# A tuned attention and feed-forward kernel: phi summed on VectorE straight from PSUM, its eps folded into a sums column, and x loaded ahead of the weights

## Chip, cores, metric

The kernel runs on one core of a Trainium2 chip. The metric is the device time of one execution in microseconds (us); lower is better. All runs quoted are fast, with a mean granted TensorE clock between 0.995 and 1.0 in every timed run. Within that band the clock and the time still go together a little: of the 31 runs of the kernel before that were timed beside the experiments, the nine at 0.997 or less have a median of 532.22 us and the 21 at 0.999 or more one of 531.42. A difference of under 1 us between two kernels is therefore not read as one here. In what follows PE is TensorE, DVE VectorE, ACT ScalarE, POOL GpSimd and SP the engine that issues the DMAs (SPq in the page's list of them).

## The reference, cut to what matters

Linear attention and a gated feed-forward layer work side by side on one layer-normalised input: 2048 tokens, D = 576, 32 heads of 18, F = 4608.

```python
xn  = layernorm(x)
q, k, v = split(xn @ wqkv)                                # 32 heads of 18
phi = lambda t: where(t > 0, t + 1, exp(t)) + 1e-6
kv  = einsum("bhsd,bhse->bhde", phi(k), v);  z = phi(k).sum(tokens)
o   = (phi(q) @ kv) / (phi(q) @ z + 1e-6)
out = x + o @ wo + (gelu(xn @ w_gate) * (xn @ w_up)) @ w_down
```

Two identities carry the kernel. First, phi(t) without its eps is max(t, 0) + exp(min(t, 0)), and min(t, 0) is -relu(-t). Second, V is never built: kv = (xn' phi(k))' Wv, so the kernel accumulates the Gram matrix G = xn' phi(k) over all tokens in PSUM.

## The kernel before

The work falls into a prologue of some 78 us (layer norm, K, Gram, Q, then kv) and a feed-forward stretch of some 450 us. The prologue is one tile loop over 16 tiles of 128 tokens, whose instructions are issued in the order of a hand-made plan of times. The kernel lays PSUM out as 8 banks (`ps_all` of 128 x 8 x 512). In the tile loop before, Gram takes banks 0 to 4, K banks 5 and 6, Q bank 7.

```python
def k_relu(n, hf=None):                       # ACT: e = relu(-k), both K banks in one (576 columns)
    ps, e, _ = k_part(n, hf)
    nc.scalar.activation(out=e, in_=ps, func=ACT.Relu, scale=-1.0)
def k_max(n, hf=None):                        # DVE: a = max(k, 0) + eps; the K banks are free after this
    ps, _, a = k_part(n, hf)
    nc.vector.tensor_scalar(out=a, in0=ps, scalar1=0.0, scalar2=EPS_ATT, op0=ALU.max, op1=ALU.add)
def k_exp(n):                                 # ACT: e = exp(-e)
    e = k_ea[n][0]
    nc.scalar.activation(out=e[:], in_=e[:], func=ACT.Exp, scale=-1.0)
def k_add(n):                                 # POOL: phi(k) = e + a, for the Gram step
    e, a = k_ea.pop(n)
    (nc.gpsimd if n < NS - 1 else nc.vector).tensor_tensor(out=pk[:, n, :], in0=e[:], in1=a[:], op=ALU.add)

G_A = {0: [...], 1: [...], 2: [...], 4: [...]}    # four of five row blocks of G in the loop, banks 0 to 4
G_B = {3: [(5, 0, 0, 288), (6, 0, 288, 288)]}     # the fifth in a pass of its own, at the end
q_banks = _Ring([7])                              # one bank for the q units of the loop
TILE = 3.34                                       # us per tile in the plan
# ...
# after the loop: q pairs (12,13) (15,16) (17,18) (14,19), then the G_B pass, its copies, z and kv
```

The step of phi(q) was like that of k, with a POOL add; some units had another form on DVE. [...] marks cuts.

## Time and profile before

| | before |
|---|---|
| time, median of 3 (range) | 532.21 us (531.52 to 532.48) |
| span of the profiled run | 529.3 us |
| first gate/up matmul, the end of the prologue | 78.43 us |
| PE / DVE / ACT / POOL busy, whole span | 98 / 49 / 27 / 13% |

The prediction below shows the page and the timeline. Two views more say where PE is held up. The first is the page's chain of work that ended last, by engine, and the second the busy time by stages: each row has the stretch in us, its length, then the busy time of an engine with its number of instructions.

```profile
PE 88%; DVE 5%; ACT 3%; POOL 1%; DMA 1%; issue 0%; SPq 0%; ACTq 0%; POOLq 0%; DVEq 0%
```

```profile
core 0: us, PE busy (x) PEld busy (x) DVE busy (x) ACT busy (x) POOL busy (x), PEclk, DMA share, GB/s
14.36:62.94 48.58, 45.60 (x340) 33.82 (x340) 39.02 (x75) 34.95 (x72) 32.24 (x33) 1.00 0.52 119
78.43:529.30 450.87, 447.18 (x3942) 261.82 (x3940) 194.59 (x280) 89.50 (x154) 24.62 (x26) 1.00 0.37 107
```

The chain leaves PE for 12% of the span, mostly through DVE, ACT and POOL, and nearly all of that lies in the prologue (from 80 us on, DVE's part of the chain is 0.1%). The first stage is the tile loop from the first Gram step to the last: DVE is busy for 39 of 48.6 us, POOL for 32. A PE figure near 94% says little here, since matmul records overlap: the Gram step at 15.96 in the prediction's first timeline ends by its record at 17.11 (15.96 + 1.15), while the next group of matmuls starts at 16.94.

### The profile page before, as it was taken

What the parts mean: (1) busy time and instruction counts of PE and PEld (TensorE: products, weight loads), DVE (VectorE), ACT (ScalarE), POOL (GpSimd) and SP (SyncE); (2) the same over time, 40 slices, a digit from 0 to 9 for tenths busy, and PEclk for the clock granted to TensorE, in tenths of its full rate; (3) what the DMA queues carried; (4) which work ended last, traced back from release to release, by engine and by line L of the source; (5) the groups of instructions that cost most, each with busy time, mean ns of one, the idle gap of its engine ahead of it and who ended that gap; (6) DMA issues with size and microseconds to landing.
All of it is one profiled execution on the core that took longest, in us unless ns stands there. A gap on an engine that the chain in (4) does not pass through costs nothing.

```text
span 529.3 us, 10714 instructions
## 1 busy us (share of the span) xinstructions
PE 518.7 (98%) x4530; PEld 315.1 (60%) x4530; DVE 257.5 (49%) x407; ACT 142.9 (27%) x266; POOL 66.7 (13%) x80
## 2 busy tenths in 40 slices
PE   7999999999999999999999999999999999999997
PEld 6766664555577764444577744444677544445775
DVE  7888683877338613433368233433485233433110
ACT  5777662232340003323200023323000123322000
POOL 3667440121002200000012000000021000000000
PEclk9999999999999999999999999999999999999999
DMA  8474205899610025555400055555100355540000
GB/s 256 118 153 122 71 1 163 246 265 267 174 53 12 24 74 146 156 154 156 135 11 13 12 163 158 143 161 150 49 22 12 101 146 161 144 134 1 12 12 24
DMA packets 106954, 57.89 MB, mean 109 GB/s; under 512 B 13402, under 2 KB 106522, under 8 KB 106906
## 3 DMA queue, kind: packets, MB, share of 16 engines
q1 hardware_dynamic: 106906, 57.21, 38.3%
q8 instruction: 35, 0.57, 0.5%
q14 instruction: 13, 0.11, 0.1%
HBM read 52.86 MB, written 2.36 MB: 104 GB/s over the span
## 4 chain that ended last, share of the span: by engine, by line
PE 88%; DVE 5%; ACT 3%; POOL 1%; DMA 1%; issue 0%; SPq 0%; ACTq 0%; POOLq 0%; DVEq 0%
PE ps_all L336 54%; PE ps_all L675 27%; PE ps_all L680 4%; DVE phi_a L409 1%; PE ps_all L306 1%; DVE xn L225 1%; DVE pqT L421 1%; PE ps_all L254 1%; POOL hT L291 1%; DMA x_sb<-in_A_x_dram 1%; ACT phi_e L279 1%; PE ps_all L366 1%; ACT phi_e L287 1%; DVE stats L215 1%; PE ps_all L472 1%; DVE phi_a L283 1%
## 5 line engine op out<-in xcount | busy, mean ns | idle before, releaser
L336 PE MATMUL ps_all<-xnT,wg 64*128 64x512 bf16 x1152 | 272.6, 376 | 0.0
L336 PE MATMUL ps_all<-xnT,wu 64*128 64x512 bf16 x1152 | 271.7, 376 | 0.0
L646 DVE TENSOR_TENSOR hT<-ps_all,gl 128x512 bf16<-128x512 f32 x144 | 99.6, 691 | 164.6 <-ACT gl L645 164.1
L645 ACT ACTIVATE gl<-ps_all 128x512 f32<-128x512 f32 x144 | 86.1, 598 | 317.2 <-PE ps_all L336 297.8
L336 PEld LDWEIGHTS <-wu 64*128 64x128 bf16 x1152 | 108.3, 94 | 66.2
L336 PEld LDWEIGHTS <-wg 64*128 64x128 bf16 x1152 | 108.3, 94 | 65.8
L675 PE MATMUL ps_all<-wd_sb,hT 128*128 128x288 bf16 x1152 | 147.0, 286 | 0.0
L675 PEld LDWEIGHTS <-hT 128*128 128x128 bf16 x1152 | 112.3, 98 | 30.6 <-issue 1.3
L496 DVE RECIPROCAL den_sb<-den_sb 126x128 f32<-126x128 f32 (+1 forms) x80 | 68.3, 911 | 0.5
L499 POOL TENSOR_TENSOR pqT<-pqT,den_sb 126x512 bf16<-126x512 bf16 (+3 forms) x25 | 24.2, 966 | 302.7 <-DVE den_sb L496 282.4
L683 DVE TENSOR_TENSOR res<-ps_all,x_sb 128x288 bf16<-128x288 f32 x32 | 14.7, 458 | 88.0 <-PE ps_all L680 88.0
L336 PE MATMUL ps_all<-xnT,wr 64*128 64x512 bf16 x288 | 55.1, 376 | 0.0
L680 PE MATMUL ps_all<-m_sb,pqT 126*128 126x288 bf16 (+1 forms) x160 | 24.9, 286 | 0.0
L336 PEld LDWEIGHTS <-wr 64*128 64x128 bf16 x288 | 14.5, 94 | 16.8 <-issue 0.7
L254 PE MATMUL ps_all<-wqkv_sb,xnT 128*128 128x288 bf16 x160 | 22.9, 286 | 1.4 <-DVE phi_a L283 1.2
L306 PE MATMUL ps_all<-hT,xn 128*128 128x288 bf16 (+3 forms) x192 | 22.4, 266 | 1.6 <-POOL hT L291 0.8
L291 POOL TENSOR_TENSOR hT<-phi_e,phi_a 128x576 bf16<-128x576 f32 x15 | 21.5, 1434 | 13.5 <-DVE phi_a L283 7.3
L306 PEld LDWEIGHTS <-xn 128*128 128x128 bf16 (+1 forms) x192 | 18.1, 101 | 6.5 <-issue 3.1
L254 PEld LDWEIGHTS <-xnT 128*128 128x128 bf16 x160 | 15.0, 98 | 7.5 <-issue 1.1
L680 PEld LDWEIGHTS <-pqT 126*128 126x128 bf16 (+1 forms) x160 | 15.5, 97 | 4.1
L419 POOL TENSOR_TENSOR pqT<-phi_e,phi_a 126x512 bf16<-126x512 f32 (+1 forms) x12 | 15.6, 1298 | 15.1 <-DVE phi_a L409 8.1
L409 DVE TENSOR_SCALAR phi_a<-ps_all 126x512 f32<-126x512 f32 (+1 forms) x20 | 13.3, 678 | 5.2 <-ACT phi_e L402 4.8
(65 smaller groups left out, 205.7 us busy)
## 6 DMA issues: line engine op xcount, KB each, us to landing
wg<-in_B_w_gate_dram SPq DMA_DIRECT2D x72, 256.0 KB, 2.9
wu<-in_B_w_up_dram SPq DMA_DIRECT2D x72, 256.0 KB, 3.5
wd_sb<-in_B_w_down_dram SPq DMA_DIRECT2D x12, 432.0 KB, 4.4
wr<-in_B_w_gate_dram SPq DMA_DIRECT2D x72, 32.0 KB, 2.7
wr<-in_B_w_up_dram SPq DMA_DIRECT2D x72, 32.0 KB, 3.0
out_dram<-res SPq DMA_DIRECT2D x15, 144.0 KB, 1.8
x_sb<-in_A_x_dram SPq DMA_DIRECT2D x3, 576.0 KB, 6.0
wqkv_sb<-in_A_wqkv_dram SPq DMA_DIRECT2D x2, 576.0 KB, 5.9
```

The costliest lines, as they stand in the source:

```text
L254: nc.tensor.matmul(ps_all[:, k_bank(n, hf), :HALF], lhsT=xnT[:, kt, n * P:(n + 1) * P], rhs=wqkv_sb[:, kt, D + hf * HALF:D + (hf + 1) * HALF],
L291: (nc.gpsimd if n < NS - 1 else nc.vector).tensor_tensor(out=pk[:, n, :], in0=e[:], in1=a[:], op=ALU.add)
L306: nc.tensor.matmul(ps_all[:m, b, col:col + w], lhsT=xn[:, n, j0:j0 + m], rhs=pk[:, n, d0:d0 + w], start=(n == 0 and col == 0), stop=(n == ...
L336: return nc.tensor.matmul(self.outs[i], lhsT=self.lhs(i, rows, kt), rhs=self.rhs(i, rows, kt), start=start, stop=stop, skip_group_check=True,)
L409: nc.vector.tensor_scalar(out=a, in0=ps, scalar1=0.0, scalar2=one + EPS_ATT, op0=ALU.max, op1=ALU.add)
L419: nc.gpsimd.tensor_tensor(out=out_, in0=e, in1=a, op=ALU.add)
L496: nc.vector.reciprocal(out=d[:, h:h + P], in_=d[:, h:h + P])
L499: nc.gpsimd.tensor_tensor(out=pqT[:rows, c, cols], in0=pqT[:rows, c, cols], in1=d, op=ALU.mult)
L645: nc.scalar.activation(out=gl[:], in_=ps_all[:, b[0], :], func=ACT.Gelu_apprx_tanh)
L646: nc.vector.tensor_tensor(out=hT[:, GUB * k + i, :], in0=ps_all[:, b[1], :], in1=gl[:], op=ALU.mult)
L675: nc.tensor.matmul(acc, lhsT=hT[:, f, j * P:(j + 1) * P], rhs=wd_sb[:, f, hs], start=(f == 0), stop=False,)
L680: nc.tensor.matmul(acc, lhsT=pqT[:rows, c, ts_], rhs=m_sb[:rows, c, hs], start=False, stop=(c == NCH - 1),)
```

## The change

The intent is to take POOL out of phi(k), to make PE the only bound of the tile loop, and to start the loop earlier. The diff, cut to its core:

```diff
-    load_x(0, 1); load_x(1, 1); load_wk(0); (last rows of wk); load_x(2, 1); load_wk(1); load_x(3, 1); load_x(4, 4)
+    load_x(0, 1); load_x(1, 1); load_x(2, 2); load_w(1); load_x(4, 2); load_x(6, 2)

-    def k_max(n, hf=None): ...  vector.tensor_scalar(max 0, + eps)
-    def k_exp(n): ...           scalar.activation on 576 columns
-    def k_add(n): ...           gpsimd.tensor_tensor(e + a)
+    def k_exp(n, hf): ...       scalar.activation on 288 columns
+    def k_sum(n, hf):
+        ps, e, out_ = k_part(n, hf)
+        nc.vector.scalar_tensor_tensor(out=out_, in0=ps, scalar=0.0, in1=e, op0=ALU.max, op1=ALU.add)

-    G_A = {0: [...], 1: [...], 2: [...], 4: [...]}           # 576 columns a row block
-    G_B = {3: [...]}
+    G_A = {0: [...], 1: [...], 4: [...]}                     # 577: pk has a column of ones
+    G_B = {2: [(5, 0, 0, 288), (6, 0, 288, 289)], 3: [(0, 0, 0, 288), (1, 0, 288, 289)]}

-    q_banks = _Ring([7])
+    q_banks = _Ring([4, 7])
+    def q_eps(i): ...           gpsimd.tensor_scalar(e * 1 + eps)
+    def q_sum(i): ...           as k_sum, from the q bank

     def g_copy(kt, pieces, on):
+        nc.vector.tensor_scalar_mul(out=eps, in0=ps_all[:m, b, col + w - 1:col + w], scalar1=EPS_ATT)
-        copy(out=g_sb[...], in_=ps_all[...])
+        (ACT Identity with bias eps, or DVE tensor_scalar_add of eps)

-    TILE = 3.34
+    TILE = 2.94                  # and all times of the plan
-    # after the loop: four q pairs, G_B pass, copies, z, kv
+    # after the loop: G_B pass 2, copies, q 12, G_B pass 3, copies, q 13, z, kv, three q pairs
```

The eps of phi(k) reaches G exactly as eps times the row sums of xn. The ones column makes these sums, and the copies out of PSUM add them. The normalised tail columns that are duplicated for the transposes are also copied on DVE instead of POOL from tile 4 on.

## The prediction

Cut is what it said of the hardware that no trace or run shows: one paragraph, with the conclusion that POOL would not hold up the new sums, and some terms that rested on it. The times that the trace before does show are these. A normalisation of 128x576 takes 0.42 to 0.43 us in nine tiles, but 0.96 to 1.71 in six, in each of which it ends 0.16 to 0.18 us after a POOL add of phi(k) does. The gate product over 128x512 from PSUM takes DVE 0.69. Over 126x512, ACT takes 0.59 from PSUM and 0.63 for an exp in SBUF, and POOL 1.27 for its two-input add; it has no one-input operation of that size.

DVE per tile after came to 3.3 us (2.8 with overlaps); the term of the two sums of k is cut from it, and the terms left make 2.4. ACT's 3.4 and 2.7 keep all their terms, but where the 0.44 of an exp came from is cut; the trace before gives 0.44 as an estimate too, since relu takes 0.651 us for 576 columns and 0.405 for 288, and exp 0.683 for 576: 0.683 - (0.651 - 0.405) = 0.437. The overlap of 0.09 shows there as well (an exp from 28.23 to 28.91, the next instruction from 28.82). The forecast itself, 7.8 + 62.5 + 3.2 = 73.5, counts PE's work and stalls and loses no term; that DVE stays under PE's 3.06 per tile rests in part on the term that is cut.

> **What bounds the kernel now.** I read the page first (busy shares, slices), then the busy time by windows, then the chain of waits and the timeline of the first 95 us.
>
> ```profile
> span 529.3 us, 10714 instructions
> PE 518.7 (98%) x4530; PEld 315.1 (60%) x4530; DVE 257.5 (49%) x407; ACT 142.9 (27%) x266; POOL 66.7 (13%) x80
> ...
> PE   7999999999999999999999999999999999999997
> ...
> DVE  7888683877338613433368233433485233433110
> ```
>
> TensorE is busy throughout; VectorE is dense only in the first six slices (some 79 us), which are the attention prologue. The timeline puts the first gate/up matmul at 78.43 us. From there to the last matmul at 525.6 us I compared start times of consecutive matmuls: only 0.1 us is without issue. The change touches nothing of that stretch's PE work, so about 451 us (529.3 - 78.4) are **fixed**. All gain must come from the first 78.4 us. Matmul busy time flatters PE there[...]; start-to-start times tell the true cost:
>
> ```profile
> 15.96 1.15 PE L306 MATMUL ps_all<-hT,xn 128*128 128x288 bf16 x10
> ...
> 16.94 0.78 PE L254 MATMUL ps_all<-wqkv_sb,xnT 128*128 128x288 bf16 x5
> ...
> 17.56 1.15 PE L306 MATMUL ps_all<-hT,xn 128*128 128x288 bf16 x10
> ...
> 58.02 1.26 PE L366 MATMUL ps_all<-xnT,wqkv_sb 128*126 128x512 bf16 x5
> ...
> 59.11 1.39 PE L254 MATMUL ps_all<-wqkv_sb,xnT 128*128 128x288 bf16 x10
> ...
> 71.94 4.09 PE L306 MATMUL ps_all<-hT,xn 128*128 128x288 bf16 x32
> ...
> 75.87 0.42 PE L442 MATMUL ps_all<-zsel,g_sb 128*126 128x126 bf16 x5
> ```
>
> Columns are start, duration, engine and line. A Gram step of 10 matmuls (2304 columns) takes 16.94 - 15.96 = 0.98 us, so 0.425 ns per column; half a K tile 0.62; a Q unit 59.11 - 58.02 = 1.09; the second Gram pass 75.87 - 71.94 = 3.93. **PE work before**, from 7.3 us on: K 16 x 1.23 = 19.6, Gram 16 x 0.98 + 3.9 = 19.6, 12 Q units 13.1, four Q pairs 7.9 (64.07 to 71.94), z and kv some 1.5, transposes 1.0: 62.7. The stretch 7.3 to 78.4 is 71.1 long, so 8.4 us are stalls and spin matmuls, of which I count some 1.5 of stall before the first Gram step, 0.8 of spin and 5.8 of stall after it. What makes the stalls is visible around 33 us:
>
> ```profile
> 29.13 1.40 POOL L291 TENSOR_TENSOR hT<-phi_e,phi_a 128x576 bf16<-128x576 f32 x1 [0.51 <-ACT rstd L221]
> ...
> 29.37 1.34 DVE L225 TENSOR_SCALAR xn<-x_sb,mv,rstd 128x576 bf16<-128x576 bf16 x1 [0.38 <-ACT rstd L222]
> ...
> 32.75 0.75 DVE L283 TENSOR_SCALAR phi_a<-ps_all 128x576 f32<-128x576 f32 x1
> ...
> 33.55 1.39 PE L254 MATMUL ps_all<-wqkv_sb,xnT 128*128 128x288 bf16 x10 [0.60 <-DVE phi_a L283]
> 33.64 1.46 POOL L291 TENSOR_TENSOR hT<-phi_e,phi_a 128x576 bf16<-128x576 f32 x1 [2.63 <-DVE phi_a L283]
> ...
> 35.15 1.15 PE L306 MATMUL ps_all<-hT,xn 128*128 128x288 bf16 x10 [0.22 <-POOL hT L291]
> ```
>
> The normalisation starts under a GpSimd add, ends when that add ends (29.37 + 1.34 = 30.71, against 0.43 when undisturbed) and delays the whole DVE queue; k_max is then late, so the K bank comes free late and PE waits, and PE waits again for the 1.4 us GpSimd add of phi(k). The same pair recurs at 42 to 47 us.
>
> [...]
>
> **The change, part by part.**
> DVE, per steady tile. Before: normalisation 0.79 (mean of 15), statistics 2 x 0.45 + 0.21, k_max 0.75, q_max 0.68, the DVE form of q's last step 0.65 on every third unit, so 0.2: 3.5. After: normalisation 0.43, statistics 1.11, [...]one q sum 0.69, the 64-column copy moved from GpSimd 0.18: 3.3. Successive DVE instructions start some 0.08 before the one ahead ends (0.59 from q_max to the next start, with duration 0.67), so I take 2.8 effective.
> ACT, per tile after: rstd 0.29 + 0.20, two relus of 0.41, two exps of 0.44[...], q 0.59 + 0.63: 3.4, less 8 overlaps of 0.09: 2.7. Before it was some 0.4 less.
> POOL: its adds of 1.43 per K tile and 1.27 per Q unit go; a one-input eps operation per Q unit comes[...]. It never feeds a Gram step again.
> PE, per tile after: K 1.23, Gram 1731 columns x 0.425 = 0.74, Q unit 1.09: 3.06. **PE becomes the bound** at 3.06, with DVE and ACT at 2.7 to 2.8, where before the disturbed chain made a pitch of some 3.67 ((60.34 - 27.30)/9 between Gram starts) against PE's 3.30.
> PE total after: K 19.6, Gram 16 x 0.74 + 2 x 3.93 = 19.7, 14 Q units 15.3, three pairs 5.9, z/kv 1.5, transposes about 1.0: 63.0, 0.3 **more** than before. The eps column adds only 1 column in 577; its eps sums and copies stand beside other PE work. Gram columns move from the tile loop to two full passes later, which removes no work but gives a filler without waits, and the q pairs now come after kv, so the copies of G hide (the 0.8 us kv wait goes).
> Prologue: the normalisation no longer stands behind statistics of x tile 2, which waited for its load and cost 1.4 us of PE time before 7.3. But the K weights now come behind four x tiles.
>
> ```profile
> GB/s 0 17 244 222 252 236 298 325 301 333 371 318 378 346 136 134 30 0 0 163 1 0 164 46 267 349 45 128 71 319 318 96 153 265 149 232 3 49 115 188
> ```
>
> This is the transfer rate per microsecond over the first 40 us. Its sum to 7 us is 1.27 MB. Four x tiles and the K weights are 4 x 0.147 + 0.664 = 1.25 MB, so K can begin at about 7.5 to 8 us, not earlier than now (7.86): the early gain is swallowed by the load, but one Q unit then fits ahead of the first Gram step.
>
> **The sum.** K starts at 7.8. PE work still to do then 62.5 (transposes of the first tile are done). Stalls and spin I expect: 1.0 before the first Gram step, 1.5 in the tile loop, 0.7 in the tail where phi of the last pairs shares ACT with the gelu table load. 7.8 + 62.5 + 3.2 = 73.5 as first gate/up matmul, against 78.4: 4.9 us less, 532.2 - 4.9 = 527.3; I say 527.4.
>
> **Rivals.** (a) The plan works perfectly and PE has nearly no stall: 71 us, total 525. For it: the plan issues at 2.94 per tile, so the other engines run ahead of PE. Against: in the kernel before a plan of 3.34 came out at 3.67. (b) The waits move: ACT takes 0.4 more per tile and more instructions[...]; DVE waits for both exps before the sum frees the K bank. The relu, exp, sum chain now holds the bank where before relu and max did, some 0.5 us longer. If PE keeps 0.25 us of stall per tile, and the tail 1.5, the total is 530 to 531. (c) K weights land late, at 9 to 9.5 us: everything shifts by 1.5, total 529. (d) The last pairs' phi holds banks that gate/up wants: three pairs need 2.2 us of ACT each against 2 us of PE, then 1.28 of table load and GpSimd's eps; a stall of 0.5 to 1.5, total 528 to 529.
>
> **Range and chances.** (a) and the more likely halves of (b) to (d) span 525.2 to 530.4, with run noise of half a microsecond. 2% is 10.6 us; all the non-work of PE in the prologue is 8.4, plus 1.4 before 7.3 that the weights' load keeps: so faster by 2% needs more than there is. Slower by 2% needs twice today's stalls. Chances: faster 0.01, within 0.98, slower 0.01.
>
> **What would show it.** Right if: the first gate/up matmul starts at 72 to 75 us; the last Gram step of the tile loop begins near 55, before it was 62.94; normalisation is about 0.43 in most tiles; [...]the Gram steps have no wait on POOL; first K matmul at 7.5 to 8.2; the stretch after it as long as before. Wrong if: gate/up starts before 71.5 or after 76.5; PE waits in most tiles for ACT's exp or DVE's sum; the normalisation is still blocked in half the tiles, by the eps operation; K starts after 9; a second ACT table load appears for the copies with a bias; or the gate/up stretch itself gains stalls.

## The result

| | before | after |
|---|---|---|
| time, median (range), 4 runs each | 531.87 (530.70 to 532.48) | 525.17 (524.61 to 526.45) |
| profiled run, its span | 531.11, 529.3 | 526.45, 524.7 |
| first gate/up matmul in the profile | 78.43 | 73.41 |
| pitch of the tile loop (mean time from one tile to the next) | 3.67 | 3.05 |

The ratio is 0.988 (95% interval 0.9854 to 0.9906). Ratios are the mean time of one kernel's fast runs over that of the other's of the same rounds, so they differ a little from the ratio of the medians. The change is 6.7 us by the medians. The result is within 2%, as predicted; it is 2.2 us under the 527.4 predicted and 0.03 us under the lower end of the range as it was written. The profiled run of the changed kernel is the slowest of its four.

The page after: span and busy time, the slices of DVE, and the chain by engine.

```profile
span 524.7 us, 10664 instructions
PE 517.2 (99%) x4502; PEld 315.8 (60%) x4502; DVE 248.4 (47%) x426; ACT 147.9 (28%) x301; POOL 40.1 (8%) x63
...
DVE  7887545977348423333388134333584233333110
...
PE 96%; DMA 2%; ACT 1%; DVE 0%; SPq 0%; issue 0%; DVEq 0%
```

PE now carries 96% of the chain, and DVE's part has gone from 5% to nothing. POOL's busy time fell from 66.7 to 40.1 us. DVE's dense part ends earlier. The stages after, in the same columns:

```profile
14.47:54.85 40.38, 39.47 (x291) 29.35 (x290) 32.77 (x91) 36.03 (x99) 6.18 (x10) 1.00 0.54 125
54.85:73.41 18.56, 18.56 (x167) 13.49 (x166) 7.71 (x20) 8.57 (x17) 3.26 (x6) 1.00 0.00 1
73.41:524.70 451.29, 447.59 (x3942) 262.79 (x3938) 197.21 (x282) 94.24 (x163) 27.05 (x30) 1.00 0.38 109
```

The loop took 8.2 us less (48.58 to 40.38). The tail took 3.1 more (78.43 - 62.94 = 15.49 before, 18.56 after), mainly because Gram columns moved into it. The feed-forward stretch is the same within 0.4 us. The sum is -5.0 us at the first gate/up matmul (the start of the first Gram step hardly moved: 14.36 to 14.47). One tile of the loop after, from its timeline (start, duration, engine, line):

```profile
40.80 0.91 PE L294 MATMUL ps_all<-hT,xn 128*128 128x288 bf16 x7
...
41.30 0.77 ACT L274 ACTIVATE phi_e<-phi_e 128x288 f32<-128x288 f32 x2
...
41.55 1.24 PE L347 MATMUL ps_all<-xnT,wqkv_sb 128*126 128x512 bf16 x5
...
41.77 0.82 DVE L278 SCALAR_TENSOR_TENSOR hT<-ps_all,phi_e 128x288 bf16<-128x288 f32 x2
...
42.67 0.62 POOL L389 TENSOR_SCALAR phi_e<-phi_e 126x512 f32<-126x512 f32 x1 [2.38 <-DVE hT L278]
...
43.85 0.91 PE L294 MATMUL ps_all<-hT,xn 128*128 128x288 bf16 x7
...
44.03 0.42 DVE L221 TENSOR_SCALAR xn<-x_sb,mv,rstd 128x576 bf16<-128x576 bf16 x1
...
46.44 0.69 DVE L393 SCALAR_TENSOR_TENSOR pqT<-ps_all,phi_e 126x512 bf16<-126x512 f32 x1 [0.79 <-POOL phi_e L389]
```

From one Gram step to the next it is 43.85 - 40.80 = 3.05 us, what PE alone needs. None of PE's lines here has a wait behind it. The two exps (41.30 to 42.07) are still at work when the first of the two sums starts at 41.77: each half waits for its own exp alone. The normalisation takes 0.42 us, and POOL does one operation of 0.62. Who PE waited for, the three largest before (first fence, from 7 us to 79) and after (second, 7 to 74): total us, times, longest.

```profile
PE ps_all L240 <- DVE xn L225: 1.3, 1, 1.3
PE ps_all L254 <- DVE phi_a L283: 1.2, 2, 0.6
PE ps_all L306 <- POOL hT L291: 0.8, 4, 0.2
```

```profile
PE ps_all L250 <- DMA wqkv_sb<-in_A_wqkv_dram: 0.8, 1, 0.8
PE ps_all L250 <- DMA xnT<-xn: 0.7, 1, 0.7
PE ps_all L236 <- ACT xnT L239: 0.6, 1, 0.6
```

The waits for DVE and POOL are gone, but for one of 0.2 us for a sum at the start of the loop. What is left are two DMA landings, which differ from run to run (the wait for the weights is 0.4 us in a_noeps and a_nocol, that for a transpose 0.3 in a_loads and none in a_nocol), and one copy before the loop. Measured by start times of consecutive matmuls, PE stood still 7.3 us before (from 7.3 to 78.4 us) and 3.2 after (from 7.3 to 73.4), of which 1.8 are the two landings (by the same measure).

### The profile page after: what moved, and what is told of

Same layout as the page of the kernel before. It is cut to its first block, busy times and chain, and to the rows that moved or that the text cites. A ratio compares the mean times of both kernels' runs of the same rounds, so it can differ in the third digit from the quotient of the medians.

```text
span 524.7 us, 10664 instructions
## 1 busy us (share of the span) xinstructions
PE 517.2 (99%) x4502; PEld 315.8 (60%) x4502; DVE 248.4 (47%) x426; ACT 147.9 (28%) x301; POOL 40.1 (8%) x63
## 4 chain that ended last, share of the span: by engine, by line
PE 96%; DMA 2%; ACT 1%; DVE 0%; SPq 0%; issue 0%; DVEq 0%
PE ps_all L318 55%; PE ps_all L664 27%; PE ps_all L669 4%; PE ps_all L294 3%; PE ps_all L250 3%; PE ps_all L347 3%; DMA wqkv_sb<-in_A_wqkv_dram 1%; DMA xnT<-xn 1%; PE ps_all L442 1%; PE ps_all L424 0%; PE ps_all L646 0%; SPq L93 0%; ACT phi_e L270 0%; DVE hT L278 0%; ACT xnT L239 0%; ACT phi_e L274 0%
## 5 line engine op out<-in xcount | busy, mean ns | idle before, releaser
L294 PE MATMUL ps_all<-hT,xn 128*128 128x288 bf16 (+4 forms) x176 | 22.4, 276 | 0.0
L393 DVE SCALAR_TENSOR_TENSOR pqT<-ps_all,phi_e 126x512 bf16<-126x512 f32 (+1 forms) x20 | 13.4, 672 | 12.4 <-POOL phi_e L389 12.4
L347 PE MATMUL ps_all<-xnT,wqkv_sb 128*126 128x512 bf16 (+1 forms) x70 | 17.4, 378 | 0.0
L389 POOL TENSOR_SCALAR phi_e<-phi_e 126x512 f32<-126x512 f32 (+1 forms) x20 | 12.4, 618 | 54.2 <-DVE hT L278 29.8
```

The source lines that it names most:

```text
L294: nc.tensor.matmul(ps_all[:m, b, col:col + w], lhsT=xn[:, n, j0:j0 + m], rhs=pk[:, n, d0:d0 + w], start=(n == 0 and col == 0), stop=(n == ...
L347: nc.tensor.matmul(ps, lhsT=wqkv_sb[:, kt, q0:q0 + rows], rhs=xnT[:, kt, sc * SC:(sc + 1) * SC], start=(kt == 0), stop=(kt == KT - 1),)
L393: nc.vector.scalar_tensor_tensor(out=out_, in0=ps, scalar=0.0, in1=e, op0=ALU.max, op1=ALU.add)
```

## The experiments

Twelve kernels, each timed in 5 rounds beside the kernel before on the same chip; all twelve passed the comparison with the reference. "Before" in the table is the median of the kernel before in the same rounds. The twelve ran in three groups on three chips. The changed kernel was not timed again beside them, so its 525.17 comes from another session; the medians of the kernel before in all sessions lie between 531.41 and 531.87.

| run | based on | time, median (range) | before | ratio (95%) |
|---|---|---|---|---|
| b_sum | before | 533.45 (532.27 to 534.06) | 531.55 | 1.0036 (1.0021 to 1.0052) |
| b_dummy | before | 534.19 (533.33 to 534.38) | 531.55 | 1.0050 (1.0035 to 1.0065) |
| b_half | before | 528.87 (528.36 to 531.30) | 531.57 | 0.9955 (0.9938 to 0.9972) |
| a_pooladd | after | 535.97 (535.52 to 538.13) | 531.55 | 1.0095 (1.0077 to 1.0114) |
| a_whole | after | 533.22 (532.80 to 533.69) | 531.57 | 1.0030 (1.0017 to 1.0043) |
| a_q1 | after | 536.12 (535.72 to 536.69) | 531.57 | 1.0085 (1.0072 to 1.0098) |
| a_wkfirst | after | 526.27 (525.09 to 526.83) | 531.55 | 0.9895 (0.9879 to 0.9912) |
| a_tail | after | 525.75 (525.50 to 526.22) | 531.41 | 0.9894 (0.9872 to 0.9916) |
| a_noeps | after | 525.24 (524.92 to 525.80) | 531.41 | 0.9882 (0.9860 to 0.9904) |
| a_nocol | after | 525.15 (524.40 to 525.47) | 531.41 | 0.9877 (0.9855 to 0.9900) |
| a_loads | after | 524.83 (524.44 to 525.74) | 531.41 | 0.9875 (0.9849 to 0.9901) |
| a_best | after | 525.45 (525.23 to 525.69) | 531.57 | 0.9884 (0.9871 to 0.9897) |

The prediction's theory was that the POOL add (through the normalisations that it holds up, 1.34 us against 0.43, and its place ahead of each Gram step) caused the loop's stalls. The first rival was the new plan.

### b_sum: the sum alone, in the kernel before

```diff
-    def k_max(...): nc.vector.tensor_scalar(out=a, in0=ps, ...)
+    def k_max(...): pass
     def k_add(n):
-        (nc.gpsimd if n < NS - 1 else nc.vector).tensor_tensor(out=pk[:, n, :], in0=e[:], in1=a[:], op=ALU.add)
+        nc.vector.scalar_tensor_tensor(out=pk[:, n, :] (viewed as two halves), in0=ps, scalar=0.0, in1=e, op0=ALU.max, op1=ALU.add)
-   k_add times [10.08, 12.33, 14.18, 16.88, ..   k_half 1: 13.33   k_relu 1: 14.06
+   k_add times [10.08, 12.13, 14.18, 16.60, ..   k_half 1: 14.20   k_relu 1: 14.93
```

> The kernel before, with one part of the change alone: phi(k) is summed by one VectorE instruction (the larger of PSUM and 0, plus exp) in the place of the GpSimd add, k_max falls away, and three times of the plan move so that no bank is overwritten before its sum. Load order, Gram columns, tail and plan pitch stay. Theory 1 (the GpSimd add was the loss: [...]its 1.4 us in front of each Gram step): the normalisation goes to 0.43 us in tiles where no q add runs, no Gram step waits for POOL, the stalls after the first Gram step fall from 5.8 to some 3 us, total 528 to 530. Rival 2 (the gain comes from the new plan: Gram columns moved out of the loop as filler, q units earlier, load order): within 0.7 us of before, the waits only change their names, since the K bank is now held until the sum instead of until k_max.

By the medians it came out 1.9 us **slower** than before, outside both expectations. Some of that may be the state of the clock: four of its six runs have 0.995 to 0.997, and the other two took 532.27 and 532.49, some 1 us over before. Either way nothing was gained. (The eps of phi(k) falls away with k_max; the result still agreed with the reference.) The normalisation was free of POOL in every tile. This is its row in the view of that source line, with the shortest, median and longest duration in ns:

```profile
L225 DVE TENSOR_SCALAR xn<-x_sb,mv,rstd x17: 312/422/431, 5.0 to 54.8; 128x576 bf16<-128x576 bf16 x15, 128x384 bf16<-128x384 bf16 x1, 128x192 bf16<-128x192 bf16 x1
```

Before, the longest was 1705. No Gram step waited for POOL either. Still the mean pitch stayed at 3.67 us, as the timeline of one tile shows:

```profile
29.31 1.39 PE L254 MATMUL ps_all<-wqkv_sb,xnT 128*128 128x288 bf16 x10 [0.18 <-DVE hT L290]
...
30.79 0.65 ACT L279 ACTIVATE phi_e<-ps_all 128x576 f32<-128x576 f32 x1 [0.74 <-PE ps_all L254]
...
31.47 0.68 ACT L286 ACTIVATE phi_e<-phi_e 128x576 f32<-128x576 f32 x1
...
32.18 0.76 DVE L290 SCALAR_TENSOR_TENSOR hT<-ps_all,phi_e 128x576 bf16<-128x576 f32 x1 [1.02 <-ACT phi_e L286]
...
32.99 1.39 PE L254 MATMUL ps_all<-wqkv_sb,xnT 128*128 128x288 bf16 x10 [0.22 <-DVE hT L290]
```

K, relu, exp, sum, and then the next K, which may only start when the sum has read the K banks: 1.39 + 0.65 + 0.68 + 0.76 plus hops (the short delays from one engine to the next, 0.20 us in all) is the 3.68 us from 29.31 to 32.99. The sum from PSUM holds the bank until after exp, where k_max had not waited for exp but run beside it (35.66 to 36.42 us, and exp 35.65 to 36.34, in one tile before). From relu's start to the end of the last reader it is 2.15 us here (30.79 to 32.94) and was 1.45 there (34.97 to 36.42). So the K bank took over as the bound. That the mean pitch is the same is a coincidence. Before, the Gram steps from 27.30 to 60.34 us lie 3.29 to 3.37 us apart, but for four gaps of 4.55, 3.65, 4.58 and 3.69, and each of the four follows a normalisation that took 1.33 to 1.71 us. In b_sum those are gone, and every gap from 30.54 to 63.51 us is 3.63 to 3.68. A wait of some 0.35 us came back in every tile: PE waited for the sum 13 times, 3.8 us in all. The theory as I stated it, that to remove these waits brings 2 to 4 us, falls. The rival's reason is right as far as this part alone goes: the waits changed their names. That POOL was behind those four long gaps before is not refuted.

### b_dummy: the same with a POOL add that nobody waits for

```diff
     def k_add(n):  (as in b_sum)
+        nc.gpsimd.tensor_tensor(out=k_ea[n][1][:], in0=k_ea[n][0][:], in1=k_ea[n][0][:], op=ALU.add)
```

> As b_sum, with an add of 576 columns on GpSimd after each sum that nobody waits for, so the GpSimd load of before without its place in front of the Gram step. [...]the normalisation is 1.3 us in about half of the tiles again and the time goes back to within 0.7 us of before. If the place of the add in the chain was what cost, the time stays within 0.7 us of b_sum though the normalisation is slow.

(The condition of the first case is that the held-up normalisation is what cost.)

The normalisation's median rose from 0.42 to 0.64 us and its longest to 1.09, so a POOL add that nobody waits for does hold it up. The sum itself was not touched: 0.75 to 0.76 us in all 16 tiles, though the POOL add starts at about the same time (35.62 against 35.51 in one tile). The time rose by 0.7 us over b_sum, and the two intervals overlap. It is 2.6 us over before, so neither expectation held as written; the first had counted on a gain in b_sum. The pitch stayed 3.67. Where the loop is bound by the K banks, a slower normalisation hides beside it. What the held-up normalisations alone cost in the kernel before, where k_max freed the banks without waiting for exp, no run isolates.

### b_half: b_sum with the bank handed back by halves

```diff
-        (k_relu, [x_, x_, x_, x_, 18.01, ..]),  (k_exp, [.., 18.73, ..]),  (k_add, [.., 19.54, ..])
+        relu, exp and sum of tiles 4 to 15 for half 0 and half 1 apart:
+        k_relu [17.39, ..] [18.01, ..], k_exph [18.27, ..] [18.73, ..], k_sumh [18.87, ..] [19.54, ..]
```

> As the run that put the sum alone into the kernel before, with relu, exp and sum of tiles 4 to 15 done in two halves, so that each K bank is free again after its own half. That run took 3.67 us per tile, and its own chain for one pair of K banks adds up to just that: K 1.40, relu 0.65, exp 0.68, sum 0.76 and four hops. Theory 3 (the sum from PSUM keeps the K bank until after exp, so it pays only where the bank is handed back by halves): the loop of one half is 0.78 + 0.41 + 0.44 + 0.46, 2.2 us with hops, under PE's 3.30; the wait of 0.35 us in each tile goes, total 529 to 531. Rival: ACT with four more instructions per tile, or DVE, holds the pitch near 3.6; total 532.5 to 534.

Theory 3 held (the half sum, 0.46 in it, takes 0.45 us here at 43.64): 528.87 us, 0.1 us under its range, 4.6 us faster than b_sum and 2.7 faster than before. (In the profiles gate/up starts 4.75 us earlier than in b_sum. Of that 3.4 lie in the loop; 1.7 lie ahead of the first Gram step, where the two kernels hardly differ.) Two starts of the K step in its timeline:

```profile
37.73 1.39 PE L254 MATMUL ps_all<-wqkv_sb,xnT 128*128 128x288 bf16 x10
...
41.03 1.39 PE L254 MATMUL ps_all<-wqkv_sb,xnT 128*128 128x288 bf16 x10
```

The pitch is 3.30 us, PE's own need with the old split of Gram. So three **more** instructions per tile than in b_sum (two on ACT, one on DVE; the four in the expectation were miscounted), which a count of engine time sees as a cost, made the loop PE-bound: from the fifth tile on all K steps are 3.29 to 3.30 us apart, but for one at 3.79. The halves with k_max and the POOL add kept were not tried.

### a_whole: the changed kernel without halves

```diff
-   k_relu / k_exp / k_sum of halves 0 and 1, tiles 4 to 15
+   k_relu_w / k_exp_w / k_sum_w on 576 columns at the later half's times (sum of tile 5 at 21.99)
```

> The changed kernel with relu, exp and sum of tiles 4 to 15 on whole tiles of 576 columns instead of halves: fewer instructions, the same sum. Theory 3: the pitch of the tile loop goes from 3.05 to the chain's 3.65 us, so some 6 us more over 11 tiles, total 530 to 533. Rival (halves are of no account since PE is the bound and the plan leaves slack): within 1 us of the changed kernel.

533.22 us, 8.0 us slower than the changed kernel and slower than the kernel before. The pitch in its timeline is 3.68 us (K starts at 39.73 and 43.41), the same chain as in b_sum. The wait that PE has:

```profile
PE ps_all L250 <- DVE hT L298: 6.0, 11, 1.2
```

Theory 3 is shown from both sides. The time is 0.2 us above the range that I had written. From the fifth tile on every K step comes 3.63 to 3.68 us after the last. The changed kernel has two shorter gaps there, 2.30 and 2.82, which lost 1.3 and 0.8 us instead of 0.62.

### a_q1: the changed kernel with one bank for q

```diff
-    q_banks = _Ring([4, 7])
+    q_banks = _Ring([7])
-        (q_unit, [11.89, 18.55, 20.85, 26.83, 29.88]), .. (q_sum, [18.00, 25.75, 28.60, 31.66, 34.72])
+        (q_unit, [11.89, 18.55, 22.02, 26.83, 29.88]), .. (q_sum, [18.00, 22.00, 25.75, 29.86, 32.80])
         (relu, exp and eps of q moved up in between)
```

> The changed kernel with one PSUM bank for the q units instead of two, as before the change, and the q steps moved up in the plan so that a bank is read before it is written again. This undoes what moving 256 Gram columns (two of five row blocks) out of the tile loop made room for. A q bank is held from the first matmul to the end of the sum: 1.26 + 0.6 relu + 0.63 exp + 0.62 eps + 0.69 sum with hops is 4.0 us at the least. Theory 4 (the longer phi chain needs the second bank): pitch of 4.0 to 4.5 us, total 535 to 541. Rival: the q unit waits beside other PE work; within 2 us of the changed kernel.

536.12 us, 11 us slower than the changed kernel. Its timeline:

```profile
42.25 1.24 PE L347 MATMUL ps_all<-xnT,wqkv_sb 128*126 128x512 bf16 x5 [1.08 <-DVE pqT L393]
...
45.81 0.69 DVE L393 SCALAR_TENSOR_TENSOR pqT<-ps_all,phi_e 126x512 bf16<-126x512 f32 x1 [1.39 <-POOL phi_e L389]
...
46.55 1.24 PE L347 MATMUL ps_all<-xnT,wqkv_sb 128*126 128x512 bf16 x5 [1.08 <-DVE pqT L393]
```

The q unit waited 8 times for its bank, 8.4 us in all, and the pitch is 46.55 - 42.25 = 4.30. In the changed kernel a bank is written at 41.55 and its sum ends at 46.44 + 0.69 = 47.13: 5.6 us, which fits only with two banks at 3.05 us each. Theory 4 held. Moving one more row block of Gram out of the loop is therefore no mere filler: it makes room for the second q bank. (The expectation's "256 Gram columns" is a slip: the one row block more is 576 columns. And with one bank the plan was mended by hand, not tuned, so 11 us is the size of the effect and not an exact price.)

### a_pooladd: the changed kernel with the POOL add back

```diff
-        nc.vector.scalar_tensor_tensor(out=out_, in0=ps, scalar=0.0, in1=e, op0=ALU.max, op1=ALU.add)
+        nc.vector.tensor_scalar(out=a, in0=ps, scalar1=0.0, scalar2=0.0, op0=ALU.max, op1=ALU.add)
+        nc.gpsimd.tensor_tensor(out=out_, in0=e, in1=a, op=ALU.add)
```

> The changed kernel with the sum of phi(k) taken apart again: VectorE takes the larger of PSUM and 0 where the sum stood, GpSimd adds exp, per half. Plan, loads and tail stay as changed. Theory 1: GpSimd is busy 1.6 us more per tile, the normalisation is blocked in many tiles, Gram steps wait for POOL; 1.5 to 4 us slower than the changed kernel. Rival 2 (the plan is what counts, with 1.2 us of slack between sum and Gram step in the steady loop): less than 0.7 us slower.

535.97 us: 10.8 us slower than the changed kernel, far beyond both expectations. The normalisation was nearly free (median 0.42 us, longest 0.82), so a held-up normalisation isn't the reason. The timeline shows what is:

```profile
37.50 1.55 POOL L280 TENSOR_TENSOR hT<-phi_e,phi_a 128x288 bf16<-128x288 f32 x2 [1.79 <-DVE phi_a L279]
...
39.13 0.62 POOL L391 TENSOR_SCALAR phi_e<-phi_e 126x512 f32<-126x512 f32 x1
...
39.78 0.69 DVE L395 SCALAR_TENSOR_TENSOR pqT<-ps_all,phi_e 126x512 bf16<-126x512 f32 x1 [1.10 <-POOL phi_e L391]
...
40.53 1.24 PE L349 MATMUL ps_all<-xnT,wqkv_sb 128*126 128x512 bf16 x5 [0.53 <-DVE pqT L395]
```

POOL took its instructions in program order here. The two K adds stand ahead of q's eps operation, whose exp had ended at 36.54; POOL stood idle until the adds could start at 37.50, and the eps operation ran at 39.13. DVE waits 1.1 us for it, in front of the next normalisation and the next max of k, for which the next K adds wait in turn. Each tile is then a ring through POOL and DVE: the q sum before had started at 35.74, and 39.78 - 35.74 is 4.04 us. PE isn't part of the ring but is held to its pitch, since it waits for the q bank (q units at 36.49 and 40.53). Two jobs that each fit on POOL don't fit one behind the other.

### a_wkfirst: K weights ahead of x tiles 2 and 3

```diff
-    load_x(2, 2); load_w(1)
+    load_w(1); load_x(2, 2)
```

> The changed kernel with the K weights issued ahead of x tiles 2 and 3, two lines swapped. In the changed kernel PE waits 1.0 us for the K weights at 7.3 us. If that load sets the start, K begins near 7.3 and gate/up starts 0.3 to 0.8 us earlier. If x of tile 2 then comes late (statistics, transposes), the wait moves to the transposes and the time is within 0.3 us of the changed kernel.

K began at 7.32 us in the profile. That is no clear gain: it is 8.24 in the profile of the changed kernel, but 7.22 to 7.86 in seven other profiles with the loads in the changed order. Then PE waited for the normalisation of tile 2:

```profile
PE ps_all L236 <- DVE xn L221: 1.3, 1, 1.3
```

The median is 526.27, 1.1 us over the changed kernel; the intervals of the ratios overlap, so the sign is likely rather than certain. From K's start to the first q unit it is 6.49 us here against 5.15 in the changed kernel. So a wait came up at the transposes, as the second expectation said, though the time is not within its 0.3 us, and no gain is seen for it. x ahead of the weights is likely the better order of these two; the old order itself was not tried in the new plan.

### a_noeps and a_nocol: the two eps devices taken away

```diff
a_noeps:  q_eps(i): -  nc.gpsimd.tensor_scalar(out=e, in0=e, ..., scalar2=EPS_ATT)   +  pass
a_nocol:  Gram 288 columns instead of 289, no eps sums, plain copies
```

> The changed kernel without the eps operation of phi(q) on GpSimd (a result wrong by one part in a million[...]). In the changed kernel VectorE stands idle 12 us in all for it. Theory: that idle time is slack, PE is the bound; within 0.5 us of the changed kernel. Rival: the eps operation delays q sums and with them the bank of the next q unit; 1 us or more faster.

> The changed kernel without the sums column and without the eps of phi(k): 288 columns instead of 289, plain copies of Gram, no small instructions for the sum (wrong by one part in a million). PE loses 80 columns, 0.03 us; the copies with a bias beside Gram cost ACT 0.1 us each. Theory: the eps column is free, within 0.3 us of the changed kernel. Rival: the copies at the end of the loop hold up z and kv, 0.5 us or more faster.

525.24 and 525.15, the changed kernel's 525.17. Both results are wrong by one part in a million on purpose, and agree with the reference within its tolerance. Neither shows a cost: the differences are under 0.1 us, with intervals of 1.2 us or more to either side. To that accuracy the 12.4 us that DVE stands waiting for POOL's eps operation are slack, and the sums column is free.

### a_tail: Gram pass, z and kv behind the q pairs again

```diff
-    (G_B pass 3, copies 2 and 3, q 13, z, kv), then three q pairs
+    (copy 2, q 13), three q pairs, then G_B pass 3, copy 3, z on banks 6 and 7, kv on 2 and 3
```

> The changed kernel with the end undone: the last Gram pass, its copies, z and kv come after the q pairs again. PE then has no work beside the copy of the last Gram columns, so kv waits for it as before (0.8 us in the kernel before), and gate/up waits for the z mask on its first bank. Theory: 0.7 to 1.5 us slower than the changed kernel. Rival: the phi work of the pairs is then hidden by the Gram pass and gives back what the wait costs; within 0.4 us.

525.75, 0.6 us over the changed kernel, between the two expectations and with overlapping intervals: inconclusive. The profile shows another wait than I expected. PE waited 0.9 us for q sums to free the banks of the Gram pass, a result of my choice of banks; the wait of kv for its copy did not appear.

### a_loads and a_best: two tries at a faster one

```diff
a_loads:  weight preloads at 18.25 + TILE * i instead of 18.0 + TILE * i
a_best:   load_x(2, 1); load_w(1); load_x(3, 1); tile 3 transposed in bank 4; its neighbour's copy ahead of an exp
```

> The changed kernel with the preloads of V and gate/up weights issued 0.25 us later in the plan, that is just behind the DMA transpose of a tile instead of just ahead of it. In the changed kernel one transpose took 4.5 us where 2.9 is the median, behind a weight load, and PE waited 0.85 us. Theory: no transpose over 3.5 us, that wait goes, and the time is 0.3 to 0.9 us shorter with less spread over runs. Rival: the transposes vary whatever is ahead of them; within 0.3 us.

> A try at a faster one, from the changed kernel: x tile 3 is loaded behind the K weights (147 KB less ahead of them, some 0.5 us), the PE transposes of tile 3 go to bank 4 so that they don't wait for the copy of tile 2, and that copy goes ahead of an exp on ACT. PE waits 0.3 to 1.0 us for the K weights and 0.8 us for that copy in the changed kernel. If both go: 523.7 to 524.6. If the copy just moves the wait to the K halves of tile 2, or x of tile 3 comes late: 524.8 to 525.5.

a_loads gave 524.83, inside the scatter of the changed kernel. A DMA transpose still took up to 4.4 us to land (the twelve took 2.6 to 4.4, median 3.0; in the changed kernel 2.6 to 4.5, median 2.9), so the order of issue doesn't explain the slow ones; what does stays open. a_best started K at 7.37 us and had the first loop q unit at 12.95. That is 5.58 us after K's start, against 5.15 in the changed kernel, so its start is no better. Its time was 525.45, no gain, and the profile has a transpose landing late again (0.74 us of idle PE at 29.1). No run here beats the changed kernel beyond doubt.

## Why the prediction was right, and where its reasons were not

**The fixed stretch** held: 450.9 us before, 451.3 after. So did the bound on any gain: 6.7 us of the 10.6 that 2% would be.

**PE's work** held. K to first gate/up lasted 73.41 - 8.24 = 65.2 us, and less 2.3 of stall that is 62.9, with two spin matmuls, against 62.5. The pitch of 3.05 was predicted as 3.06, and the last Gram step of the loop began at 54.85 ("near 55").

**The costs of the new instructions**: normalisation 0.42 (predicted 0.43); the sums of k 0.45 for 288 columns and those of q 0.67 to 0.69 for 512 (0.69 predicted); the eps operation on POOL 0.62, the mean of 20, four of them on 72 partitions (the estimate was higher; it came at no cost that a_noeps could show). That POOL does not hold up the sums is shown by b_dummy alone: 0.75 to 0.76 us in all 16 tiles beside its adds.

**K's start**: 8.24 in the profile of the changed kernel, just out of the 7.5 to 8.2 given, but 7.22 to 7.86 in the seven other profiles with the same order of loads. PE's wait for the weights varies: 0.8 us in this profile, 0.4 in a_noeps and a_nocol, none listed in a_tail.

**The size.** The profiled pair gives 5.0 us at gate/up against 4.9 predicted, and the medians give 6.7 against 4.8. The mis-sized term is "Stalls and spin I expect: 1.0 before the first Gram step, 1.5 in the tile loop, 0.7 in the tail". Measured after K's start: 0.8 before the first Gram step; 1.3 in the loop of which 0.85 is one late transpose, so 0.45 where it lands in time, as in a_nocol; 0.1 in the tail. The loop and the tail had been given some 1.5 us too much. In the profile of a_nocol the last three q pairs start at 65.85 us, against 67.53 in the profile of the changed kernel, with the same work in front of them: this is the size of the scatter, to which PE's listed waits for DMA landings add 1.1 us (1.5 in the changed kernel, 0.4 in a_nocol), and the changed kernel's profiled run was its slowest. That its 5.0 us meets the 4.9 predicted is in part luck: K began 0.4 us later and PE's work was 0.4 us longer than said, and stalls and spin were 0.9 us shorter. Without the late landings it comes near rival (a), nearly no stall and a total of 525: a_nocol's gate/up starts at 71.73 us, and 525 is where the medians lie.

**The cause.** Here a step failed, though the number did not. I wrote that the normalisation "delays the whole DVE queue; k_max is then late, so the K bank comes free late and PE waits, and PE waits again for the 1.4 us GpSimd add", and concluded "PE becomes the bound" from the sums of engine time. What this says of the kernel before stands as far as the trace goes: all four long gaps there follow a blocked normalisation. The conclusion doesn't follow from it: b_sum takes these waits away and is no faster. What decided here whether PE could be the bound is how long a PSUM bank is held. The sum from PSUM lengthens that hold (2.15 us from relu's start in b_sum, 1.45 before), and the change pays for it with two things that I had booked otherwise. The halves I counted as ACT's cost of 0.4 us per tile; they are worth 4.6 us in the old plan (b_half against b_sum) and 8.0 in the new one (a_whole). The second Gram pass I called "a filler without waits"; it frees the bank without which the loop runs at 4.30 us (a_q1). Rival (b) named the longer hold of the bank and its half a microsecond, but as a risk. It took DVE to wait "for both exps before the sum", and did not see that with halves each sum waits for its own exp alone. What POOL's add alone cost before stays open: b_sum removes it and lengthens the hold in one step, and an add on DVE with k_max kept was not run.

**The parts don't add.** Each of the sum, the halves and the second q bank, taken out alone, costs 8 to 11 us, more than the whole gain of 6.7; the sum put in alone gains nothing. They belong together. (The undoing runs keep the changed kernel's plan but for the moves shown, so a plan tuned for each might lose less.) Of the gain, b_half's two parts account for 2.7 us. Between the profiles of b_half and the changed kernel lie another 3.3 us up to gate/up (76.71 to 73.41): stalls after the first Gram step fall from 3.7 to 1.5 us; one q unit more, 1.1 us, is done before that step, which starts 0.3 us earlier; PE's work is 0.3 us more. Which line of the plan earns which part of this, the runs don't say.

## What to carry to other kernels

When an operation is fused to read PSUM later, work out anew how long the bank is held: matmul, every step up to the last reader, and the hop back. Where that sum over the number of banks exceeded the pitch that was hoped for, the fusion alone gained nothing here: 3.48 us and four hops for the K banks as a whole went with a pitch of 3.68 (b_sum, a_whole), and 4.0 at least for one q bank with 4.30 (a_q1), against 3.05 with enough banks. Halving the pieces or freeing another bank can be worth more than the instructions they add (4.6 and 8.0 us for the halves, 11 for the bank). And before two jobs share an engine that takes them in program order, as POOL did in a_pooladd, ask what the second one's reader holds while the first one runs.
